# The gate of a gated unit as one silu on ScalarE in place of tanh and a VectorE product

## The chip, the cores and the metric

One core of a Trainium2 chip runs the whole program. The metric is the device time of one execution in microseconds (us), the median of several. Five engines work side by side, each through its own list in order: PE (TensorE, matrix products), DVE (VectorE), ACT (ScalarE), POOL (GpSimd) and SP (SyncE, which issues most DMAs).

## The reference

Three layers, one after the other, over 8 x 3072 = 24576 rows of 256 numbers:

```python
X = np.fft.rfft(x, axis=1)
y = np.fft.irfft(X * (filt_r + 1j * filt_i)[None], n=3072, axis=1)
...
out[do_compute] = xc + gate_w * (relu(xc @ w1[e]) @ w2[e])
...
rms = np.sqrt(np.mean(x * x, axis=-1, keepdims=True) + 1e-06)
xn = x / rms * rms_g
g = xn @ w_gate
silu = g * (1.0 / (1.0 + np.exp(-g)))
val = xn @ w_val
return (silu * val @ w_out).astype(np.float32)
```

The first layer is a filter by a Fourier transform, the second sends rows to one of eight experts, and the third, the gated unit with 1536 hidden channels, takes every row. The change lies in the third.

## The kernel before

The program has three stages: transform and routing, then the experts, then the gated unit (`glu`). `glu` takes the rows in 32 blocks of 768 and the hidden channels in 6 pairs of 256, so there are 192 pairs of work.

A pair makes two first products, g for the gate and v for the value, by a scheme of Winograd that needs seven products p1 to p7 of half size for each. Each product is three matmuls of fp16 parts (L1587) with 384 columns. They are summed in two kinds of PSUM bank: `psa` (p1, and on it p6, p7, p4; three buffers) and `psb` (p2 by itself, and p5 with p3 on it; two buffers). The quarters c11, c12, c22, c21 of a result arise on the way, and a further product may be added to a bank only when what was in it has been read:

- `copy` (L1594, ACT) takes p1, p5 and p1 + p6 out of their banks as s1, s5 and u2. p6 may go on p1 only after the first copy, p3 on p5 after the second, p7 after the third.
- `plus` (L1598, DVE) makes c11 = p2 + s1, c12 = (p5 + p3) + u2 and c22 = (p1 + p6 + p7) + s5 (rows gc<- or vc<-). p4 may go on its bank only after c22; then the bank holds c21.
- `gate` (L1603, ACT) makes t = tanh(g / 2) into a tile `th` of three buffers, and `gate2` (L1609, DVE) makes g = (1 + t) * g. For c21 the gate reads the bank.
- `hidden` (L1617, DVE) makes v * scale * g, `high` (L1627, ACT) its upper fp16 part hh, `low` (L1630, POOL) the lower one hl.

The second product (`stage_b`, L1674) multiplies hh and hl with the output weights, three matmuls of 256 columns for each of 12 groups of a pair, 18 slots behind the first. `finish` (L1687, ACT) takes a block's result out.

Beside this, `row_ops` makes the next block's rows: six squares on ACT (L777, first pair of a block), 1 / rms in tiny steps on DVE (L779, then L130, L132, L138, L139, L141 of `rsqrt_ops`), scalings on both (L790, L793), four sums on POOL (L804), the upper parts on ACT (L807), the lower on DVE (L809), and a transposing DMA (L812).

The order on each engine is written out by hand, slot by slot. 14 slots are a pair: a slot is one product, what follows it, one group of the second product, and a piece of the next rows. `place` gives the slots of the products (g: 0, 2, 3, 4, 5, 6, 8; v: 7, 9, 10, 11, 12, 13, 15 in the order p1 p2 p5 p6 p3 p7 p4; 15 lies in the next pair), and `plan` those of what follows:

```python
for n, k in (("c11", 4), ("c12", 7), ("c22", 8), ("c21", 9)):
    plan[k].append((gate, n))
    plan[k + 2].append((gate2, n))
for n, k in (("c11", 11), ("c12", 14), ("c22", 15), ("c21", 16)):
    plan[k].append((hidden, n))
    plan[k + 2].append((high, n))
    plan[k + 3].append((low, n))
```

An engine runs its list in this order, and an instruction that waits holds up all behind it on its engine.

Of the kernel before, what the change touches and what calls it, by code (L numbers as in the profile page):

```python
# [36 lines left out]
# the first expert's first AHEAD rows are fixed after FREEZE batches  # L37
# [4 lines left out]
def shape_constants():  # L42
    """Tables that depend on the shapes alone: the factors of the 3072-point
    transform (96 x 32), signs of the mirrored half, token numbers."""
# [54 lines left out]
    # tokens of a route step: transposed columns (n, t) in groups of 128  # L99
# [21 lines left out]
def rsqrt_ops(nc, pool, out, v, iters):  # L121
    """out ~ v ** -0.5 (v > 0): a bit-level first guess (3.5% off) and Newton steps; a list of
    instructions to emit in this order"""
# [28 lines left out]
def colsum(nc, psp, ones, v, n, tag="misc"):  # L152
    """Sum over the partitions of v [p, n], the same on every partition."""
    ps = psp.tile([128, 512], F32, tag=tag, name="colsum")
    nc.tensor.matmul(out=ps[:, :n], lhsT=ones[: v.shape[0]], rhs=v, start=True, stop=True)
    return ps[:, :n]


def fft_route(tc, x, filr, fili, w9, consts, y_dram, lst, lp, front, shared, then):
    """y_dram, lst, shared["basee"] from x; then: the parts of what comes next, taken one by one between  # L160
    the instructions of the steps behind the last of the first stage, which count from 0 on in
    shared["step"]. The pool front is theirs from 0 on, the left side's memory from 6 on; shared
    also has a pool and one of PSUM for small things."""
# [9 lines left out]
    with ExitStack() as ctx:  # L173
# [50 lines left out]
        # but for the first row of the lower half (in the first group) the halves are the same  # L224
# [21 lines left out]
        # every other group's matrix of the inverse is the transposed one of the forward  # L246
# [22 lines left out]
        # the places in the lists, of the batches until FREEZE and of the others  # L269
# [27 lines left out]
        # one-hot rows and a group of zeros behind them  # L297
# [86 lines left out]
        def stage1(s):  # L384
            """rows (k1, re/im) of the 96-point transforms -> DRAM"""
# [31 lines left out]
        def stage23(s):  # L417
            """32-point transforms, the filter, the inverse 32-point ones"""
# [46 lines left out]
        def stage4(s):  # L465
            """back to tokens"""
# [22 lines left out]
        def batch_scale(b):  # L489
            """s with |y| * s <= 60000: |y| <= max|F| * ||x_b||"""  # L490
# [15 lines left out]
        def route(s):  # L506
# [97 lines left out]
            def place():  # L604
# [12 lines left out]
                # the first expert's later tokens come behind its first AHEAD rows  # L617
# [42 lines left out]
        for s in range(steps + lagr + 3):  # L660
# [19 lines left out]
            # behind the last transforms nothing else hides the routes' waits  # L680
# [25 lines left out]
def split(nc, hi, lo, src, scale):  # L706
    """hi + lo = src * scale in two fp16 parts"""
    nc.scalar.activation(out=hi, in_=src, func=ACTF.Copy, scale=scale)
    nc.vector.scalar_tensor_tensor(
        out=lo, in0=src, scalar=scale, in1=hi, op0=ALU.mult, op1=ALU.subtract  # L710
    )


def decode64_ops(nc, pool, out, w):
    """out [128, n] = float64 values given as words w [128, n, (low, high)], rounded to float32
    (zero below its normal range); a list of instructions to emit in this order"""
# [7 lines left out]
        # sign, exponent and 20 bits  # L724
# [10 lines left out]
        # and the other 32  # L735
# [8 lines left out]
# The GLU's two products with the rows, C = A B, are made per pair of halves of the rows (A1, A2),  # L744
# of the channels and of 256 columns by Winograd's form of Strassen's scheme:
#   s1 = a21 + a22, s2 = s1 - a11, s3 = a11 - a21, s4 = a12 - s2
#   t1 = b12 - b11, t2 = b22 - t1, t3 = b22 - b12, t4 = b21 - t2
#   c11 = a11 b11 + a12 b21, u2 = a11 b11 + s2 t2, u3 = u2 + s3 t3
#   c12 = u2 + s1 t1 + s4 b22, c21 = u3 + a22 t4, c22 = u3 + s1 t1
# PA: the products' places in the order a22 a11 a12 s1 s2 s3 s4 (t4 b11 b21 t1 t2 t3 b22)  # L750
PA = dict(p1=1, p2=2, p3=6, p4=0, p5=3, p6=4, p7=5)
GH = 384
# slots between a pair's first product and its first in the second
BEHIND = 18
# slots by which the second block's rows come later than another block's
LATE = 14
# the slots of a block's steps towards the next one's rows: squares, 1 / rms (and how many apart),
# scalings (by whom: ScalarE or VectorE), sums, and per third the fp16 parts and what is left
# [8 lines left out]
def row_ops(nc, pool, x, xa, xs, xT, jk):  # L767
    """rows x [128, 6, D] over their rms, times XG (the first three of a partition are A1, the
    others A2) -> the seven factors in the tiles xa ([128, 3, 8, 128] or three of a third of it),
    their fp16 parts in xs, transposed  # L770
    in xT [128, 14 (hi, lo), GH]; a list of (slot of a block, instruction)"""
# [13 lines left out]
    # places of xa: a21, then those of PA  # L785
# [31 lines left out]
def block_list(nc, cp, basee, c_blk):  # L817
    """expert counts -> list of (expert, first slot) per block of TL slots behind every expert's
    first NSE blocks; the number of pairs of them; a list of instructions to emit in this order"""
# [28 lines left out]
    def loads():  # L848
# [16 lines left out]
        # n // 3 = n * 171 >> 9 for n < 512  # L865
# [11 lines left out]
        # the first block of an expert  # L877
# [13 lines left out]
        # entries behind the last block: the rows of the list that hold no token  # L891
# [16 lines left out]
def moe(tc, y_dram, lst, c_blk, w1, w2, wsp, lp, front, shared):  # L908
    """NSE blocks of TB list rows for every expert (rows without a token do nothing), then a
    loop over blocks of TL of what is left. The parts until the last yield make the first two  # L910
    blocks' rows and the first expert's weights and belong between the last steps of fft_route;
    after them shared["glu"] is what the GLU has to have made on the way."""
# [6 lines left out]
    # nothing before step n  # L919
# [32 lines left out]
    # the list of blocks from NS on: 0: expert, 1: row  # L952
# [13 lines left out]
    # a scale for w1 and one for w2 from their norms, to 0.2% (undone exactly in the end), and  # L966
    # the products' scale in 12
# [55 lines left out]
    with ExitStack() as ctx:  # L1023
# [5 lines left out]
        # ids of the next block but one  # L1029
        ids_n = cp.tile([128, 4, 2], I32, name="m_ids_n")  # L1030
        jk_x = cp.tile([128, D], F16, name="m_jkx")
        # state that goes from one turn of the loop to the next, empty at first
# [34 lines left out]
        # blocks from NS on come from the list  # L1067
# [12 lines left out]
        # n: sums of squares of the rows -> r: 1 / rms, to 0.2% (undone exactly in the end)  # L1080
# [27 lines left out]
        def stage_a(d, w_, f, T, busy=False):  # L1108
# [11 lines left out]
            # the sum is at most 16 XS TBIG  # L1120
# [37 lines left out]
        # tokens per partition in block j  # L1158
# [3 lines left out]
        # what block j does in its slot f for the blocks behind it  # L1162
        def step(j, u, f):
# [25 lines left out]
            # the first block's come late  # L1189
# [12 lines left out]
        # the next expert's weights  # L1202
# [14 lines left out]
        # what VectorE and ScalarE can do beside the block's own work in a slot, and what the  # L1217
        # weights take of it, in us
# [6 lines left out]
        def block(j, u, w, wp):  # L1225
# [4 lines left out]
            # GpSimdE still fills the lists in the first block  # L1230
# [74 lines left out]
        # the list of the blocks from NS on and the GLU's weights and first rows are made on the way  # L1305
        work, late, credit = [], [], [0.0, 0.0]

        def begin():
# [3 lines left out]
            # what they need is loaded some slots ahead  # L1312
# [9 lines left out]
        # the loop's first block ends one without tokens  # L1322
# [19 lines left out]
def glu_weights(gp, wg, wv, wo, rg):  # L1342
    """wg and wv (times rg) as the fp16 parts of the seven factors and wo as fp16 parts, under
    scales from their norms, and the first block's rows, in tiles of gp; w["work"](nc, ctx, tc,
    ps_m) lists (us, instruction) that make the weights, w["first"](nc, y_dram, room) then
    instructions for the rows"""
# [23 lines left out]
    def make(nc, ctx, tc, ps_m):  # L1370
# [34 lines left out]
        def scale(m, part):  # L1405
            """st 8-10: squares of norms; 11-13: 1 / norm; 14-16: scales; 17-19: inverses"""
# [26 lines left out]
        def columns(m, n, w):  # L1433
            pieces(m, [w[k * 128:(k + 1) * 128, c * 256:(c + 1) * 256]
                       for k in range(2) for c in range(NP)])
            # a column's norm is at most that of the rows' largest values
# [10 lines left out]
            # a factor is at most sqrt(8) times the norm  # L1447
# [51 lines left out]
        # 20: tanh's scale  # L1499
        one(20, 17, 0.5 / XG)  # L1500
        # h = (1 + tanh) * g * (v * st21) = silu * v * st22, at most TBIG
        mul(22, 11, 12)
        one(22, 22, 0.9 * TBIG / 256.0)
        mul(21, 17, 18)
        mul(21, 21, 22)
        one(21, 21, 0.5 / (XG * XG))
        # 23: the output's scale
# [7 lines left out]
def glu_rows(dram, i):  # L1515
    """(partitions, places, rows [partitions, places, D]) of block i; the first block has the
    tokens of the first step of the routes, which are among the first 768 of every list"""
# [11 lines left out]
def glu(tc, y_dram, w, out, ntok=NTOK):  # L1529
# [5 lines left out]
    with ExitStack() as ctx:  # L1535
# [32 lines left out]
        def stage_a(i, q):  # L1568
            """{slot: product}, {slot: what follows in it}"""
# [6 lines left out]
            # p1 + p6 + p7 + p4 and p5 + p3 are sums in one bank, read on the way  # L1576
# [23 lines left out]
            def gate(n):  # L1600
                z["t", n] = tile_("th", bufs=3)
                src = z["g", "p1" if n == "c21" else n]
                nc.scalar.activation(out=z["t", n], in_=src, func=ACTF.Tanh, scale=st[:, 20:21])  # L1603

            def gate2(n):
                src = z["g", "p1" if n == "c21" else n]
                if n == "c21":
                    z["g", n] = tile_("gc21")
                v.scalar_tensor_tensor(  # L1609
                    out=z["g", n], in0=z["t", n], scalar=1.0, in1=src, op0=ALU.add, op1=ALU.mult  # L1610
                )

            def hidden(n):
# [164 lines left out]
```

## Time and profile before

| | us |
|---|---|
| median of 3 runs | 3460.76 |
| lowest, highest | 3455.25, 3463.61 |
| span of the profiled execution, first to last instruction | 3426.4 |
| busy in the span: PE | 3207.6 (94%) |
| DVE | 2682.2 (78%) |
| ACT | 2284.5 (67%) |
| POOL | 1565.2 (46%) |

For the profiled execution the span is listed, and no total of its own; the runs' median is 34.4 us above that span. The shares are means over three stages of different kind: what the change does is read from the last one. A matmul's row begins when it starts to stream and ends, by a model, when its last result is out, so rows of neighbouring matmuls overlap. The granted clock of 1.00 is TensorE's upper level, 2.4 GHz.

### The profile page before, as it was taken

To read this page: it belongs to the slowest core of one execution; us is meant where nothing else is said; L and a number is where in the kernel's file an instruction comes from. 1 tells how busy PE (TensorE), PEld (TensorE's weight loads), DVE (VectorE), ACT (ScalarE), POOL (GpSimd) and SP (SyncE) were. 2 spreads that over 40 slices of the span, in tenths; PEclk is the share of its full clock that TensorE was granted. 3 is DMA by queue.
4 is the path that set the end of the run, shared out by engine and by line. 5 is a ranking of instruction groups with operands and counts; after the bars stand their busy time and mean duration, and the time that the engine had idled before them with its cause. 6 is when DMAs were issued, how large, how long until landed. Compare 5 with 4: busy or idle time off the path is not lost.

```text
span 3426.4 us, 61356 instructions
## 1 busy us (share of the span) xinstructions
PE 3207.6 (94%) x21784; PEld 2173.9 (63%) x21784; DVE 2682.2 (78%) x5587; ACT 2284.5 (67%) x4949; POOL 1565.2 (46%) x1546
## 2 busy tenths in 40 slices
PE   7888888889989988999999999999999999999999
PEld 3455555455555665666666666666666666666666
DVE  3666777698988656888888888888888888888886
ACT  5555655667676755776767777776677767767665
POOL 2355556756565643344343444334334443434433
PEclk8999998899999999999999999999999999999999
DMA  9999998555555462112111111111211111111110
GB/s 266 268 259 261 272 260 229 163 167 158 172 162 176 140 179 64 45 41 55 41 45 46 45 45 46 50 45 41 55 36 47 44 50 45 46 50 45 41 37 19
DMA packets 377758, 364.77 MB, mean 106 GB/s; under 512 B 264036, under 2 KB 323444, under 8 KB 373094
## 3 DMA queue, kind: packets, MB, share of 16 engines
q1 hardware_dynamic: 360502, 335.29, 35.8%
q0 software_dynamic: 16944, 25.51, 2.6%
q8 instruction: 173, 2.83, 0.3%
q14 instruction: 139, 1.14, 0.1%
HBM read 157.96 MB, written 133.80 MB: 85 GB/s over the span
## 4 chain that ended last, share of the span: by engine, by line
PE 52%; DVE 6%; ACT 2%; issue 1%; DMA 0%; DVEq 0%; POOL 0%; ACTq 0%; SPq 0%
PE psa L1587 19%; PE o L1674 18%; PE psb L1587 15%; DVE gc L1609 3%; DVE vc L1598 2%; ACT th L1603 1%; ACT s L1594 1%; DVE rsq_g L132 1%; DVE vc L1617 1%; DVE gc L1598 0%; PE m_o L1133 0%; DMA x<-y 0%; DMA xT<-xs 0%; DVE ss L779 0%; ACT hh L1627 0%
## 5 line engine op out<-in xcount | busy, mean ns | idle before, releaser
L1630 POOL TENSOR_TENSOR hl<-vc,hh 128x384 f16<-128x384 f32 x768 | 735.6, 961 | 1238.2 <-ACT hh L1627 1238.2
L1674 PE MATMUL o<-g_wo,hh 128*128 128x256 f16 x4608 | 878.9, 273 | 0.0
L1674 PEld LDWEIGHTS <-hh 128*128 128x128 f16 x4608 | 450.5, 98 | 296.8
L1674 PE MATMUL o<-g_wo,hl 128*128 128x256 f16 x2304 | 628.0, 273 | 0.1
L1627 ACT CAST hh<-vc 128x384 f16<-128x384 f32 x768 | 392.7, 511 | 162.4 <-DVE vc L1617 155.9
L1587 PE MATMUL psa<-xT,g_vhi 128*128 128x384 f16 x1488 | 484.1, 326 | 15.7 <-DVE vc L1598 15.6
L1587 PE MATMUL psa<-xT,g_ghi 128*128 128x384 f16 x1488 | 484.2, 326 | 0.8 <-DMA xT<-xs 0.5
L1617 DVE SCALAR_TENSOR_TENSOR vc<-vc,g_st,gc 128x384 f32<-128x384 f32 x576 | 405.5, 725 | 0.0
L1609 DVE SCALAR_TENSOR_TENSOR gc<-th,gc 128x384 f32<-128x384 f32 x576 | 392.4, 708 | 0.0
L1587 PE MATMUL psb<-xT,g_vhi 128*128 128x384 f16 x1116 | 363.0, 326 | 11.4 <-ACT s L1594 11.4
L1587 PEld LDWEIGHTS <-g_ghi 128*128 128x128 f16 x2688 | 263.1, 98 | 123.1 <-issue 0.3
L1603 ACT ACTIVATE th<-gc,g_st 128x384 f32<-128x384 f32 x576 | 338.5, 615 | 0.0
L1587 PE MATMUL psb<-xT,g_ghi 128*128 128x384 f16 x1116 | 332.8, 326 | 0.0
L1115 PE MATMUL psa<-m_xT,m_w 128*128 128x512 f16 (+1 forms) x1344 | 318.7, 377 | 10.1 <-DMA m_xT<-m_xs 8.7
L1587 PEld LDWEIGHTS <-g_vhi 128*128 128x128 f16 x2688 | 262.7, 98 | 102.6
L1133 PE MATMUL m_o<-m_w,m_hh 128*128 128x256 f16 x1740 | 304.8, 277 | 11.7 <-PEq L1336 10.1
L1594 ACT COPY s<-psb 128x384 f32<-128x384 f32 x384 | 183.5, 478 | 171.1 <-PE psb L1587 171.1
L1594 ACT COPY s<-psa 128x384 f32<-128x384 f32 x384 | 182.9, 476 | 164.5 <-PE psa L1587 164.4
L1133 PE MATMUL m_o<-m_w,m_hl 128*128 128x256 f16 x870 | 241.2, 277 | 44.2 <-POOL m_hl L1126 32.2
L1587 PE MATMUL psa<-xT,g_glo 128*128 128x384 f16 x744 | 242.5, 326 | 0.0
L1674 PEld LDWEIGHTS <-hl 128*128 128x128 f16 x2304 | 225.4, 98 | 26.7 <-POOL hl L1630 0.6
L1587 PE MATMUL psa<-xT,g_vlo 128*128 128x384 f16 x744 | 242.4, 326 | 0.0
(255 smaller groups left out, 6521.2 us busy)
## 6 DMA issues: line engine op xcount, KB each, us to landing
x<-in_x_dram SPq DMA_DIRECT2D x64, 384.0 KB
a_d<-a SPq DMA_DIRECT2D x64, 384.0 KB
a<-a_d SPq DMA_DIRECT2D x128, 192.0 KB
b_d<-bt SPq DMA_DIRECT2D x128, 192.0 KB
b<-b_d SPq DMA_DIRECT2D x32, 768.0 KB
y<-y SPq DMA_DIRECT2D x64, 384.0 KB
x<-y SPq DMA_DIRECT2D x28, 768.0 KB
out_dram<-ot SPq DMA_DIRECT2D x27, 768.0 KB
```

The costliest lines, as they stand in the source:

```text
L132: lambda: ve.tensor_scalar(out=g, in0=g, scalar1=-1.0, scalar2=float(0x5F3759DF), op0=ALU.mult, op1=ALU.add),
L1115: nc.tensor.matmul(out=ps, lhsT=w[:, k, fs], rhs=d["xT"][:, o + k, 0:n], start=(j == 0), stop=(j == 5),)
L1133: nc.tensor.matmul(out=o[t // 2][:, t % 2, :], lhsT=h[:, ts_], rhs=w_["w2"][:, f, i, :], start=(f == k == t % 2 == 0), stop=(f == KF - 1 a ...
L1587: nc.tensor.matmul(out=ps, lhsT=w_[m][:, q, k, :], rhs=xT[:, o + k, :], start=(j == 0 and bank == p), stop=(j == 2), skip_group_check=True,)
L1594: nc.scalar.copy(out=z[m, n], in_=z[m, p])
L1598: v.tensor_tensor(out=z[m, n], in0=z[m, p], in1=z[m, b], op=ALU.add)
L1603: nc.scalar.activation(out=z["t", n], in_=src, func=ACTF.Tanh, scale=st[:, 20:21])
L1609: v.scalar_tensor_tensor(out=z["g", n], in0=z["t", n], scalar=1.0, in1=src, op0=ALU.add, op1=ALU.mult)
L1617: v.scalar_tensor_tensor(out=z["v", n], in0=src, scalar=st[:, 21:22], in1=z["g", n], op0=ALU.mult, op1=ALU.mult,)
L1627: nc.scalar.copy(out=part(hh, n), in_=z["v", n])
L1630: nc.gpsimd.tensor_tensor(out=part(hl, n), in0=z["v", n], in1=part(hh, n), op=ALU.subtract)
L1674: nc.tensor.matmul(out=o_t[b][:, t % 2, :], lhsT=h[:, f, ts_], rhs=wo16[:, 2 * q + f, k, :], start=(j == 0 and q == 0 and n == first_of[b] ...
```

## The change

The gate becomes one ScalarE activation, silu(g) = g * sigmoid(g), written over g (for c21 into the same tile as before). The tanh, its tile `th` and the VectorE product are gone. The scalars beside it change with it: silu takes the whole argument, so its scale is twice tanh's, and the factor st21 of `hidden` no longer carries g's scale. In the listing after, lines behind the gate lie up to eight higher: `copy` is L1593, `plus` L1597, `hidden` L1609 and `high` L1619.

```diff
-        # 20: tanh's scale
-        one(20, 17, 0.5 / XG)
-        # h = (1 + tanh) * g * (v * st21) = silu * v * st22, at most TBIG
+        one(20, 17, 1.0 / XG)
         mul(22, 11, 12)
         one(22, 22, 0.9 * TBIG / 256.0)
-        mul(21, 17, 18)
-        mul(21, 21, 22)
-        one(21, 21, 0.5 / (XG * XG))
+        mul(21, 18, 22)
+        one(21, 21, 1.0 / XG)
...
             def gate(n):
-                z["t", n] = tile_("th", bufs=3)
-                src = z["g", "p1" if n == "c21" else n]
-                nc.scalar.activation(out=z["t", n], in_=src, func=ACTF.Tanh, scale=st[:, 20:21])
-
-            def gate2(n):
                 src = z["g", "p1" if n == "c21" else n]
                 if n == "c21":
                     z["g", n] = tile_("gc21")
-                v.scalar_tensor_tensor(
-                    out=z["g", n], in0=z["t", n], scalar=1.0, in1=src, op0=ALU.add, op1=ALU.mult
-                )
+                nc.scalar.activation(out=z["g", n], in_=src, func=ACTF.Silu, scale=st[:, 20:21])
...
                 plan[k].append((gate, n))
-                plan[k + 2].append((gate2, n))
```

On VectorE, in the first pair of a block where the 1 / rms of the next rows begins, the order before (with the semaphores that each instruction waits for):

```order
L1609 SCALAR_TENSOR_TENSOR gc_25118<-th,gc_25118 128x384 [waits Activation_49]
L1598 TENSOR_TENSOR vc_25190<-psb,s_25168 128x384 [waits PE_49,Activation_49,Pool_49]
L1609 SCALAR_TENSOR_TENSOR gc_25148<-th,gc_25148 128x384 [waits Activation_49]
L1609 SCALAR_TENSOR_TENSOR gc_25157<-th,gc_25157 128x384 [waits Activation_49]
L1609 SCALAR_TENSOR_TENSOR gc_25214<-th,psa 128x384 [waits Activation_49]
L1617 SCALAR_TENSOR_TENSOR vc_25190<-vc_25190,g_st,gc_25118 128x384 [waits DVE_49]
L779 TENSOR_SCALAR ss<-ss 128x6 [waits Activation_49]
L130 TENSOR_SCALAR rsq_g<-ss 128x6 [waits DVE_49]
L1598 TENSOR_TENSOR vc_25225<-psb,u_25212 128x384 [waits PE_49,Activation_49,Pool_49]
L132 TENSOR_SCALAR rsq_g<-rsq_g 128x6 [waits DVE_49]
L138 TENSOR_TENSOR rsq_a<-rsq_g 128x6 [waits DVE_49]
L1598 TENSOR_TENSOR vc_25235<-psa,s_25202 128x384 [waits PE_49,Pool_49]
```

and at the same place in the change:

```order
L1597 TENSOR_TENSOR vc_24657<-psb,s_24637 128x384 [waits PE_49,Activation_49,Pool_49]
L1609 SCALAR_TENSOR_TENSOR vc_24657<-vc_24657,g_st,gc_24589 128x384 [waits DVE_49]
L779 TENSOR_SCALAR ss<-ss 128x6 [waits Activation_49]
L130 TENSOR_SCALAR rsq_g<-ss 128x6 [waits DVE_49]
L1597 TENSOR_TENSOR vc_24688<-psb,u_24677 128x384 [waits PE_49,Activation_49,Pool_49]
L132 TENSOR_SCALAR rsq_g<-rsq_g 128x6 [waits DVE_49]
L138 TENSOR_TENSOR rsq_a<-rsq_g 128x6 [waits DVE_49]
L1597 TENSOR_TENSOR vc_24698<-psa,s_24668 128x384 [waits PE_49,Pool_49]
```

The four products of L1609 before are gone, and everything behind them keeps its place relative to the rest.

On ScalarE, behind the upper part L807 of the next rows in a later pair, the order before:

```order
L807 CAST xs<-xa 128x896
L1594 COPY s_20514<-psa 128x384 [waits PE_49]
L1603 ACTIVATE th<-gc_20494,g_st 128x384 [waits DVE_49]
L1603 ACTIVATE th<-gc_20504,g_st 128x384 [waits DVE_49,Activation_49]
L1603 ACTIVATE th<-psa,g_st 128x384 [waits DVE_49,PE_49]
L1594 COPY s_20547<-psb 128x384 [waits PE_49]
L1594 COPY u_20556<-psa 128x384 [waits PE_49]
```

and in the change:

```order
L807 CAST xs<-xa 128x896
L1593 COPY s_20239<-psa 128x384 [waits PE_49,Activation_49]
L1603 ACTIVATE gc_20220<-gc_20220,g_st 128x384 [waits DVE_49]
L1603 ACTIVATE gc_20230<-gc_20230,g_st 128x384 [waits DVE_49]
L1603 ACTIVATE gc_20260<-psa,g_st 128x384 [waits PE_49]
L1593 COPY s_20269<-psb 128x384 [waits PE_49,Activation_49]
L1593 COPY u_20277<-psa 128x384 [waits PE_49,Activation_49]
```

The gates stand where they stood and wait for less; 867 of the 1152 copies now also wait for an earlier instruction of ScalarE itself. At the start of the unit the order has one instruction more:

```order
L1593 COPY u_15548<-psa 128x384
L1603 ACT_TABLE_LOAD
L1603 ACTIVATE gc_15537<-gc_15537,g_st 128x384
L1593 COPY s_15565<-psa 128x384
L1603 ACTIVATE gc_15554<-gc_15554,g_st 128x384
```

That load is the only one in the unit; before, the whole program has one, at its beginning.

## Rows read from the trace of the kernel before

**Rows 1.** Windows: stretch and length, busy PE, PEld, DVE, ACT, POOL, clock, DMA.
```profile
1400.00:3300.00 1900.00, 1873.91 (x13470) 1316.77 (x13469) 1586.55 (x2967) 1344.19 (x3024) 783.61 (x804) 1.00 0.18 46
3285.00:3293.00 8.00, 8.00 (x60) 5.67 (x59) 6.00 (x13) 7.59 (x21) 2.17 (x4) 1.00 0.00 0
```

**Rows 2.** Lines by form, DVE, 1400 to 3300: busy us, mean ns, idle before.
```profile
L1609 DVE SCALAR_TENSOR_TENSOR gc<-th,gc 128x384 f32<-128x384 f32 x518 | 352.9, 708 | 0.0
```

**Rows 3.** Lines by form, ACT, 1400 to 3300.
```profile
L1603 ACT ACTIVATE th<-gc,g_st 128x384 f32<-128x384 f32 x518 | 304.5, 615 | 0.0
```

**Rows 4.** Who waited for whom, PE, 1400 to 3300: total us, times, longest.
```profile
PE psa L1587 <- DVE vc L1598: 15.1, 30, 0.8
PE psb L1587 <- ACT s L1594: 10.6, 28, 0.9
```

**Rows 5.** Chain in order of time, last block: start us, us, what.
```profile
3382.39 0.97 PE psb L1587 x6
...
3403.90 0.97 PE psb L1587 x6
```

**Rows 6.** Timeline, PE: one product, and the same one a block later.
```profile
3251.73 0.33 PE L1587 MATMUL psb<-xT,g_ghi 128*128 128x384 f16 x1
...
3317.69 0.33 PE L1587 MATMUL psb<-xT,g_ghi 128*128 128x384 f16 x1
```

**Rows 7.** Timeline, all engines, first pair of that block.
```profile
3291.80 0.48 ACT L1594 COPY u<-psa 128x384 f32<-128x384 f32 x1
3291.88 0.32 PE L1587 MATMUL psb<-xT,g_vhi 128*128 128x384 f16 x1
3292.41 0.51 ACT L1627 CAST hh<-vc 128x384 f16<-128x384 f32 x1
3292.44 0.17 DVE L130 TENSOR_SCALAR rsq_g<-ss 128x6 int32<-128x6 int32 x1
3292.55 0.56 DVE L1598 TENSOR_TENSOR vc<-psb,u 128x384 f32<-128x384 f32 x1
3293.00 0.91 POOL L1630 TENSOR_TENSOR hl<-vc,hh 128x384 f16<-128x384 f32 x1 [4.64 <-ACT hh L1627]
3293.02 0.92 DVE L132 TENSOR_SCALAR rsq_g<-rsq_g 128x6 int32<-128x6 int32 x1
3294.05 0.55 DVE L1598 TENSOR_TENSOR vc<-psa,s 128x384 f32<-128x384 f32 x1
3294.66 0.32 PE L1587 MATMUL psa<-xT,g_vhi 128*128 128x384 f16 x1 [0.50 <-DVE vc L1598]
```

**Rows 8.** Timeline, ACT and PE, two pairs later.
```profile
3302.96 0.48 ACT L1594 COPY u<-psa 128x384 f32<-128x384 f32 x1 [0.25 <-PE psa L1587]
3304.26 0.51 ACT L1627 CAST hh<-vc 128x384 f16<-128x384 f32 x1 [0.82 <-DVE vc L1617]
3311.14 0.94 ACT L807 CAST xs<-xa 128x896 f16<-128x896 f32 x1 [1.43 <-POOL xa L804]
3313.84 0.47 ACT L1594 COPY s<-psb 128x384 f32<-128x384 f32 x1
3314.36 0.32 PE L1587 MATMUL psb<-xT,g_vhi 128*128 128x384 f16 x1 [0.36 <-ACT s L1594]
```

**Rows 9.** Timeline: releases by PE of DVE and ACT, and of PE.
```profile
3289.37 0.33 PE L1587 MATMUL psb<-xT,g_vhi 128*128 128x384 f16 x1
3289.84 0.56 DVE L1598 TENSOR_TENSOR vc<-psb,s 128x384 f32<-128x384 f32 x1 [1.07 <-PE psb L1587]
3307.16 0.33 PE L1587 MATMUL psb<-xT,g_ghi 128*128 128x384 f16 x1
3307.52 0.48 ACT L1594 COPY s<-psb 128x384 f32<-128x384 f32 x1 [0.80 <-PE psb L1587]
3308.14 0.33 PE L1587 MATMUL psb<-xT,g_ghi 128*128 128x384 f16 x1
```

**Rows 10.** Timeline, ACT, start of the program.
```profile
0.73 1.28 ACT L401 ACT_TABLE_LOAD   x1 [0.73 <-PEq L1767]
```

## The prediction, made before the changed kernel was run

> **What bounds the kernel now.** I read the busy times by stage first, then who waited for whom on PE, then the timeline of one block. The change touches only the gated unit, which fills the last three fifths of the span. In its steady part [rows 1] PE is busy for 1873.9 of 1900 us at a granted clock of 1.00, DVE for 1586.6 and ACT for 1344.2. So the unit is bound by PE, and all that a lighter DVE can give back is time in which PE is not streaming. The waits of PE [rows 4] name 15.1 us for DVE (30 times) and 10.6 us for ACT (28 times): once each per block of rows.
>
> How much is lost in all comes from the pace. Two pairs that nothing disturbs take 3403.90 - 3382.39 = 21.51 us, so 10.755 a pair and 64.53 for the six of a block [rows 5]. A block that also prepares the next one's rows takes 3317.69 - 3251.73 = 65.96 [rows 6]. Each of the 31 such blocks (the last prepares nothing) loses 1.43 us, 44 us together. This is more than the waits listed, since after a wait PE also has to refill: 10.755 us for 42 matmuls of 384 and 36 of 256 columns make 0.163 for one of the first kind, while its row is 0.33 long [rows 7]. In a stream the rest lies under the next matmul; after a wait 0.16 is lost besides. The wait of 0.50 ahead of 3294.66 costs 0.66.
>
> **Where the 1.43 us arise.** First place [rows 7]: PE's p4 of the value half waits for VectorE's sum at 3294.05, which stands behind the tiny L132 of the rsqrt. L132 is 0.92 us long and ends 0.03 after POOL's hl at 3293.00, though its neighbour L130 of the same size takes 0.17: it is held by POOL. Second place [rows 8]: p3 waits for ACT's copy at 3313.84 to 3314.31. ACT was late because L807 waited 1.43 us for POOL's sums; that costs PE the wait of 0.36 and the same 0.16 of refill, 0.52. The other 0.25 are small delays around both.
>
> **The change part by part.** PE, POOL and SP keep their instructions and their order. (a) *768 products (1 + t) * g leave VectorE*, three in four of them from SBUF at 708 ns in the mean [rows 2], 353 us in the steady part. That lies beside PE, and is worth only what it takes from the two places.
>
> Second place: POOL's chain begins with hl of c11, which needs ACT's hh at 3304.26. That hh waited 0.82 for VectorE's hidden product, which stood behind three of the removed products. Without them it follows copy u, which ends at 3303.44 [rows 8]. POOL's chain, L807 and the copy start about 0.8 earlier. The lateness is 0.52, so it goes: -0.52 x 31 = **-16.1** (0 if POOL's chain does not follow, -16.1 at most).
>
> First place: the sum cannot start before L132 ends, and L132 ends with POOL's hl. hl follows hh at 3292.41, which follows copy u (end 3292.28, the earliest that hh can gain is 0.13, and about 0.24 where neighbours on ACT overlap). L132 itself can come 0.2 earlier at best, since the sum ahead of it needs PE's matmul of 3291.88 (end 3292.20, release 0.14 as in [rows 9], so 3292.34 in place of 3292.55). Both move by nearly the same amount, and POOL was ahead by 0.02 and stays so. So I take the wait as shortened, not gone: -0.2 x 31 = **-6.2**; its ends are 0 and -0.66 x 31 = -20.5. The Trainium skill (SBUF — State Buffer, SBUF: two separate sides) says that of such a pair whichever starts first holds the port for the whole instruction; by it the end is decided by these hundredths, and -20.5 would hold if L132 came first. The row of L132 agrees with it.
>
> Small delays: of the 0.25 I take half, -0.12 x 31 = **-3.7** (0 to -7.8).
>
> (b) *Silu in place of tanh, 768 times.* The operands are the same, the result goes to g itself. No row has a silu; the nearest is tanh of the same shape at 615 ns [rows 3], and I take **0** more. The lower end is the plain copy's 0.48 us [rows 9], the upper end tanh's time twice.
>
> (c) *One table load*, ahead of the first silu, where ACT has little ahead and PE waits soon: 1.28 us in the only row there is [rows 10], **+1.3**. By the Trainium skill (ScalarE: Activation LUTs, What ACT_TABLE_LOAD costs) a switch has a drain of about 1.38 us besides, so 2.66; the row shows the load alone, with nothing in flight ahead of it. By the page the sum would be 1.4 us less of a gain.
>
> (d) *A second wait on ACT's copies.* In the order of the change 867 of the 1152 copies out of PSUM wait for PE and for ACT itself, where each waited for PE alone. What ACT is waited for lies far back; the cost is that two waits release later. ACT's copy at 3307.52 started 0.03 after PE's last matmul (3307.16 + 0.33), VectorE's sum with several waits at 3289.84 started 0.14 after its own (3289.37 + 0.33) [rows 9]: 0.11 more. It hurts where a copy has little slack: the copy that ends at 3308.00 releases p3 of the gate half at 3308.14, and the release takes 0.05 (3314.31 to 3314.36, [rows 8]), so the slack is 0.09. That leaves 0.02 in each of 192 pairs, 3.8 us; VectorE's row has more waits than ACT's will, so I take half, **+2** (0 to 0.11 x 192 = 21). What is queued behind the copies on ACT are gates and casts, and PE waits for the copies alone.
>
> (e) One scalar product less in the constants: a 1-column VectorE instruction in the stage before, under PE's work there, 0; without that cover below 0.2.
>
> Sum: -16.1 - 6.2 - 3.7 + 1.3 + 2 = **-22.7 us**. The profile's span of 3426.4 would be 3403.7. The profiled execution's total time is not listed; between its span and the median of 3460.76 lie 34.4 us, which I leave as they are: 3438 us, 0.66% less. About 0.3% (10.4 us) is what a measurement of this kernel can tell from no change.
>
> **The rivals.**
> *L132 gets ahead of POOL.* Then the first place gives 20.5 in place of 6.2 and the time is 3460.8 - 37 = **3424**. For it: the two are within 0.05 us by the working above. Against it: POOL is ahead in this block by 0.02, and 30 waits of 0.50 in the mean [rows 4] say the same of the others.
> *The gain is given back at the copies.* If the second wait costs its full 0.11 in each pair, (d) is 21 and the time **3457**; if POOL's chain does not come earlier, -16.1 falls out and it is **3454**. Both end within 0.3%. For it: the slack of 0.09 is in every pair, and POOL's own work ahead of L807 stays as long as it is. Against it: the slack is there, and hh is named as waiting for VectorE.
> *Silu is longer than tanh, and ACT becomes the bound.* In the first pair of a block ACT has squares and outputs besides and is busy for 7.59 of 8 us [rows 1]; four gates lie in that stretch ahead of the value half's copy for p3. Each added x delays PE by 4x per block: with x of 0.18 the 22.7 are gone (4 x 31 x 0.18 = 22.3), and with x of 0.6, twice tanh, the time is 3438 + 74 = **3512**. For it: there is no row of a silu. Against it: copy and tanh of one shape are only 0.14 apart [rows 3, 9]. The Trainium skill (ScalarE: Activation LUTs, Step-by-step) has one element per cycle for every function, by which x is 0; no run here shows it.
> *The change does not do what it says*: if silu, square and copy needed different tables, loads would come in turn, six squares a block between gates. The order has one load in the whole unit, so this has no share of its own.
>
> **How the numbers follow.** My forecast 0.50; L132 first 0.26; given back 0.17; ACT as the bound 0.07. The range is 3416 to 3452: the forecast with the ends of its small terms, and the first rival with 8 us below it, where small delays go too. Faster by over 0.3% 0.79, within 0.3% 0.14, slower 0.07.
>
> **What would show it.** In the profile after: PE's wait for ACT's copy near each block's L807 gone, and L807's wait for POOL under 1 us; PE's wait for VectorE's vc sum still there once a block at about 0.3 (gone: the first rival); DVE busy near 60% in the steady part (83% now); silu from SBUF at 615 ns; one table load more; blocks at 65.2 us. Wrong would be: blocks of 65.9 or more, waits of PE for the copies in each pair, or gates above 0.7 us.

## The result, and the profile after

The changed kernel takes 3434.68 us (median of 4 runs, 3429.15 to 3438.36); the kernel before takes 3462.19 in the runs beside it (4 runs, 3455.25 to 3465.99). The ratio is 0.9917, with an interval of 0.9901 to 0.9933. It is faster by 27.5 us, where 22.7 were forecast, and the time lies 3.3 us below the forecast of 3438.

First the busy times by stage, over the same stretch as in [rows 1] (stretch and length, then busy PE, PEld, DVE, ACT and POOL, the granted clock, DMA):

```profile
1400.00:3300.00 1900.00, 1891.16 (x13639) 1333.77 (x13637) 1219.98 (x2305) 1340.17 (x3068) 762.17 (x815) 1.00 0.19 46
```

DVE has lost 367 us of its 1587, PE has gained 17, and ACT is where it was. The granted clock is at its upper level in both. So only a small part of the work taken from VectorE comes back, and to see where, one reads who waited for whom (us in all, times, longest). After the change, first PE, then ACT:

```profile
PE psa L1586 <- DVE vc L1597: 8.6, 30, 0.6
...
ACT xs L807 <- POOL xa L804: 14.9, 29, 0.8
ACT hh L1619 <- DVE vc L1609: 10.8, 30, 0.6
```

The same two waits of ACT in the kernel before:

```profile
ACT hh L1627 <- DVE vc L1617: 138.5, 204, 1.5
...
ACT xs L807 <- POOL xa L804: 40.8, 28, 2.1
```

Of PE's two waits of [rows 4] the one for ACT's copy is gone, and the one for VectorE's sum is shortened from 15.1 to 8.6 us. On ACT, L807's wait for POOL is 0.5 us a block, where it was 1.4 to 1.5.

The timeline of a block's first pair, all engines, at the place of [rows 7] (start, us, engine, line, operation; in brackets the idle time before and what ended it):

```profile
2318.69 0.48 ACT L1593 COPY u<-psa 128x384 f32<-128x384 f32 x1
2319.04 0.17 DVE L130 TENSOR_SCALAR rsq_g<-ss 128x6 int32<-128x6 int32 x1
2319.05 0.54 ACT L1619 CAST hh<-vc 128x384 f16<-128x384 f32 x1
2319.66 0.92 POOL L1622 TENSOR_TENSOR hl<-vc,hh 128x384 f16<-128x384 f32 x1 [4.42 <-ACT hh L1619]
2319.73 0.87 DVE L132 TENSOR_SCALAR rsq_g<-rsq_g 128x6 int32<-128x6 int32 x1
2320.72 0.56 DVE L1597 TENSOR_TENSOR vc<-psa,s 128x384 f32<-128x384 f32 x1
2321.33 0.32 PE L1586 MATMUL psa<-xT,g_vhi 128*128 128x384 f16 x1 [0.28 <-DVE vc L1597]
```

L132 still takes 0.87 us for six numbers per partition, and still ends within 0.02 of POOL's hl (2320.60 and 2320.58). The sum ahead of p4 starts 1.06 after hl's start, as it did before (1.05). What moved is hl: it starts 0.97 after the start of copy u, where it was 1.20. PE's wait is 0.28 in place of 0.50.

The timeline of ACT two pairs later, at the place of [rows 8]:

```profile
2329.69 0.48 ACT L1593 COPY u<-psa 128x384 f32<-128x384 f32 x1 [0.31 <-PE psa L1586]
2330.07 0.52 ACT L1619 CAST hh<-vc 128x384 f16<-128x384 f32 x1
...
2336.94 0.94 ACT L807 CAST xs<-xa 128x896 f16<-128x896 f32 x1 [0.50 <-POOL xa L804]
...
2339.64 0.47 ACT L1593 COPY s<-psb 128x384 f32<-128x384 f32 x1
```

The cast hh follows copy u at once, where it waited 0.82. L807 starts 7.25 after copy u (8.18 before), and the copy that p3 waits for is 0.93 earlier with it. 0.52 were lost there, so nothing is left of that wait.

The gate itself, lines by form on ACT in that stretch (count, then busy us and mean ns):

```profile
L1603 ACT ACTIVATE gc<-gc,g_st 128x384 f32<-128x384 f32 x525 | 308.8, 616 | 0.0
```

Silu takes 616 ns where tanh took 615 [rows 3]. And the start of the unit on ACT, with the one new table load:

```profile
1336.09 0.48 ACT L1593 COPY u<-psa 128x384 f32<-128x384 f32 x1
1336.59 1.28 ACT L1603 ACT_TABLE_LOAD   x1
1337.88 0.62 ACT L1603 ACTIVATE gc<-gc,g_st 128x384 f32<-128x384 f32 x1
```

**What the total is made of.** This execution took 3432.34 us and its span is 3430.5: 1.9 us lie around a span. The profile of before has a span of 3426.4, so its execution took about 3428, less than any of the listed runs of that kernel. The unit explains it: its first matmul starts at 1302.88 in the profile before and at 1333.55 in the one after. From there to the end it takes 3426.4 - 1302.88 = 2123.5 before and 3430.5 - 1333.55 = **2097.0 after, 26.5 less**. The two stages in front, which the change does not touch, took 31 us more in the second execution, and two spans compared as they stand would have shown a slower kernel. In the rest of this document I compare the length of the unit, and the period of a block by the distance of two L132: 65.97 before, 65.15 after (medians).

### The profile page after: what moved, and what is told of

It reads as the page before. It is cut to its first block, busy times and chain, and to the rows that moved or that the text cites. A ratio compares the mean times of both kernels' runs of the same rounds, so it can differ in the third digit from the quotient of the medians.

```text
span 3430.5 us, 61136 instructions
## 1 busy us (share of the span) xinstructions
PE 3211.9 (94%) x21784; PEld 2179.3 (64%) x21784; DVE 2257.9 (66%) x4818; ACT 2260.9 (66%) x4950; POOL 1529.9 (45%) x1546
## 4 chain that ended last, share of the span: by engine, by line
PE 56%; ACT 3%; DVE 1%; DMA 0%; issue 0%; DVEq 0%; SPq 0%; ACTq 0%
PE psa L1586 21%; PE o L1665 20%; PE psb L1586 16%; ACT gc L1603 1%; ACT jk L777 1%; DVE vc L1597 1%; ACT s L1593 1%; ACT hh L1619 0%; DVE rsq_g L132 0%; ACT ot L1678 0%; ACT u L1593 0%; DMA x<-y 0%; PE m_o L1133 0%; DMA xT<-xs 0%; DVE ss L779 0%
## 5 line engine op out<-in xcount | busy, mean ns | idle before, releaser
L1622 POOL TENSOR_TENSOR hl<-vc,hh 128x384 f16<-128x384 f32 x768 | 700.3, 915 | 1247.3 <-ACT hh L1619 1247.3
L1619 ACT CAST hh<-vc 128x384 f16<-128x384 f32 x768 | 394.2, 513 | 14.1 <-DVE vc L1609 13.9
L1609 DVE SCALAR_TENSOR_TENSOR vc<-vc,g_st,gc 128x384 f32<-128x384 f32 x576 | 379.2, 681 | 5.7
L1593 ACT COPY s<-psa 128x384 f32<-128x384 f32 x384 | 183.0, 477 | 296.3 <-PE psa L1586 296.2
L1603 ACT ACTIVATE gc<-gc,g_st 128x384 f32<-128x384 f32 x576 | 338.7, 616 | 0.0
L1593 ACT COPY s<-psb 128x384 f32<-128x384 f32 x384 | 183.5, 478 | 201.9 <-PE psb L1586 201.7
L1597 DVE TENSOR_TENSOR vc<-psb,s 128x384 f32<-128x384 f32 x192 | 106.6, 555 | 197.1 <-PE psb L1586 195.1
```

The source lines that it names most:

```text
L1593: nc.scalar.copy(out=z[m, n], in_=z[m, p])
L1597: v.tensor_tensor(out=z[m, n], in0=z[m, p], in1=z[m, b], op=ALU.add)
L1603: nc.scalar.activation(out=z["g", n], in_=src, func=ACTF.Silu, scale=st[:, 20:21])
L1609: v.scalar_tensor_tensor(out=z["v", n], in0=src, scalar=st[:, 21:22], in1=z["g", n], op0=ALU.mult, op1=ALU.mult,)
L1619: nc.scalar.copy(out=part(hh, n), in_=z["v", n])
L1622: nc.gpsimd.tensor_tensor(out=part(hl, n), in0=z["v", n], in1=part(hh, n), op=ALU.subtract)
```

## The experiments

The experiments ran on three chips, each with runs of the kernel before on it. The table has all of them; ratios are to the kernel before on the same chip. Unit and block are in us, each from one profiled execution.

| kernel | median, before beside it | ratio [interval] | unit | block |
|---|---|---|---|---|
| before, once more | 3441.24, 3439.86 | 1.0003 [0.9993, 1.0013] | 2123.5 | 65.97 |
| silu, and a product | 3437.94, 3439.86 | 0.9989 [0.998, 0.9999] | 2122.9 | 65.97 |
| tanh in silu's place | 3413.05, 3439.86 | 0.9913 [0.9898, 0.9928] | 2096.4 | 65.15 |
| before, one product earlier | 3441.87, 3467.58 | 0.9922 [0.9902, 0.9941] | 2097.6 | 65.15 |
| after, 1 / rms later | 3436.98, 3439.86 | 0.9993 [0.9984, 1.0002] | 2123.4 | 66.00 |
| before, 1 / rms later | 3489.12, 3467.58 | 1.0062 [1.0043, 1.0081] | 2142.4 | 66.6 |
| before, one product earlier and 1 / rms later | 3468.09, 3467.58 | 0.9998 [0.9987, 1.0009] | 2122.7 | 66.0 |
| after, L132 earlier | 3395.98, 3438.18 | 0.989 [0.9871, 0.9908] | 2083.5 | 64.71 |
| before, product and L132 earlier | 3426.07, 3438.18 | 0.9963 [0.9949, 0.9977] | 2111.5 | 65.63 |

### The kernel before, once more

No edit.

> The kernel before, unchanged, to see where its 3460 us lie: the profile read for the prediction has a span of 3426.4 us and was taken to have 34 us around it, while the changed kernel's runs have their total only 1.9 us above their span. If the 34 us lie around the span, the unit starts near 1303 us as in the profile before and the total is 34 us above the span. If that profile was of an execution with a short first stage, the unit starts near 1330 us, the total is 2 us above the span, and the unit itself takes 2123 us in both.

The total of its profiled execution is 3441.79 at a span of 3439.9, again 1.9 apart. The unit starts at 1316.36, 13.5 later than in the first profile, and takes 2123.5, the same to 0.1. So what lies around the span is small, and what differs between executions of one program lies in the stages ahead of the unit. Most of that goes with the chip: the kernel before has medians of 3438, 3440 and 3468 us on the three.

### Silu with a product behind it

The gate writes silu into a tile of its own, and VectorE makes src * 0 + silu at the place of the old product: the same operation, shape and order as before, with the function of the change on ScalarE. The lines are shown against the kernel before; the scalars are those of the change.

```diff
-                nc.scalar.activation(out=z["t", n], in_=src, func=ACTF.Tanh, scale=st[:, 20:21])
+                nc.scalar.activation(out=z["t", n], in_=src, func=ACTF.Silu, scale=st[:, 20:21])
...
-                    out=z["g", n], in0=z["t", n], scalar=1.0, in1=src, op0=ALU.add, op1=ALU.mult
+                    out=z["g", n], in0=src, scalar=0.0, in1=z["t", n], op0=ALU.mult, op1=ALU.add
```

> The changed kernel with silu written to a tile of its own and a VectorE product of the old size put back (0 * g + silu, two slots behind the gate). If the gain comes from VectorE's queue alone, both waits of PE return: blocks of 65.96 us, a total within 0.3% of the kernel before. If silu itself, the single table load or the lighter waits of the gates gave part of it, the total stays below, at 3435 to 3450 us.

The gain is gone: 2122.9 us of unit against 2123.5. Both waits of PE are back at their sizes of [rows 4]; waits of PE and of ACT, 1400 to 3300:

```profile
PE psa L1586 <- DVE vc L1597: 14.3, 29, 0.5
PE psb L1586 <- ACT s L1593: 11.0, 29, 0.9
...
ACT xs L807 <- POOL xa L804: 42.1, 29, 2.0
```

So the gain does not come from the other function, but goes with VectorE's product. One part of ScalarE's side is undone here too: the copies start 0.04 us after PE's last matmul, as in the kernel before, where most of them take 0.09 after the change. This run alone does not part that second wait from the product; the run with one product moved does, since its copies also start after 0.04.

### Tanh in silu's place

The changed kernel with the name of the function alone exchanged, so that the gate is tanh(g) and no product follows (the factor g is left out).

```diff
-                nc.scalar.activation(out=z["g", n], in_=src, func=ACTF.Silu, scale=st[:, 20:21])
+                nc.scalar.activation(out=z["g", n], in_=src, func=ACTF.Tanh, scale=st[:, 20:21])
```

> The changed kernel with tanh in place of silu (the gate is then tanh of the scaled g, without the product with g). If silu costs what tanh costs, blocks are 65.15 us and the total is that of the changed kernel, 3435 us, less 1.3 us for the table load that is not needed. If silu's rows are longer, this is faster by 4 x 31 x the difference.

A block takes 65.15 us with either function, and the unit 2096.4 against 2097.0. This kernel has one ScalarE instruction less, the table load. So silu costs what tanh costs, and the load of 1.28 us costs the unit 0.6 at most. At the end of the second pair nothing of it is left: PE begins the value half's p4 of the second pair 20.53 us after the unit's first matmul with the load (1354.08 - 1333.55) and 20.55 without (1338.23 - 1317.68).

### Before, with one product moved

Is it the 367 us of work, or the place of one product a pair behind that work? This is the kernel before with tanh, all products and their order, but with the hidden product of c11 at slot 9, ahead of three gate products, in place of slot 11 behind them.

```diff
+            plan[9].append((hidden, "c11"))
...
-                plan[k].append((hidden, n))
+                if n != "c11":
+                    plan[k].append((hidden, n))
```

> The kernel before with the hidden product of c11 two slots earlier, ahead of three of the four products (1 + t) * g; VectorE's work is the same. If PE's wait for ACT's copy arises because this product starts POOL's chain late, the wait goes: 0.52 x 31 = 16 us less, 3445 us, and L807's wait for POOL falls from 1.4 to about 0.6 us. If it is VectorE's load beside POOL that slows POOL's sums, L807 still waits 1.4 us and the total is that of before.

The block takes 65.15 us and the unit 2097.6: all but 0.6 us of the change's gain, with VectorE still busy for 1550 of 1900 us. VectorE's timeline in a pair, and below it the waits of PE and ACT, 1400 to 3300:

```profile
2319.19 0.56 DVE L1598 TENSOR_TENSOR vc<-psb,s 128x384 f32<-128x384 f32 x1 [1.07 <-PE psb L1587]
2319.78 0.62 DVE L1617 SCALAR_TENSOR_TENSOR vc<-vc,g_st,gc 128x384 f32<-128x384 f32 x1
2320.32 1.02 DVE L1609 SCALAR_TENSOR_TENSOR gc<-th,gc 128x384 f32<-128x384 f32 x2
2321.25 0.55 DVE L1609 SCALAR_TENSOR_TENSOR gc<-th,psa 128x384 f32<-128x384 f32 x1
```

```profile
PE psa L1587 <- DVE vc L1598: 8.5, 29, 0.8
...
ACT xs L807 <- POOL xa L804: 14.7, 29, 0.5
ACT hh L1627 <- DVE vc L1617: 11.0, 30, 0.5
```

The hidden product stands right behind the sum that it needs. The wait of hh for it, 138.5 us in 204 times in the kernel before, falls to 11.0 in 30, POOL's chain comes earlier, and with it L807 and the copy: the chain that the prediction gave for the second place, moved by its first link alone. I had expected only that place to be gained; the first is shortened too, since the same hh sets hl there. L132 starts 0.38 after hl in this kernel, takes 0.56 and again ends with it, and the sum starts 1.06 after hl's start, as before and after the change.

### Three ways of moving the 1 / rms that gained nothing

If POOL's hl holds L132 up, then steps of 1 / rms that come two slots later should miss it. The edit is one number, made in the changed kernel, in the kernel before, and in the kernel before with the product moved:

```diff
-RMS, APART = 11, 0.5
+RMS, APART = 13, 0.5
```

> The changed kernel with the tiny rsqrt steps two slots later (RMS 13), so that VectorE makes the sum that p4 waits for before it comes to L132, which POOL holds. If what is left of PE's wait for VectorE is POOL's hold on L132, that wait (0.28 listed, 0.43 lost per block) is gone: blocks of 64.7 us and a total 13 us lower, 3422 us. If the wait is VectorE's load or release, it stays and the total stays at 3435 us.

> The kernel before, tanh and product kept, with the rsqrt steps two slots later. If PE's wait for VectorE there is POOL's hold on L132 and not the 768 products, this wait goes without the change: 0.66 x 31 = 20 us less, 3440 us, while the wait for ACT's copy stays at 0.36 a block. If it is the load of the products, the wait stays and the total is that of before.

> Both moves on the kernel before, with tanh and all products kept. If the 768 products cost nothing beside PE and mattered only by their two places, this loses as little as the changed kernel with its rsqrt steps later: blocks of 64.8 us, 3425 us or less. If VectorE's load matters in itself, it stays above the changed kernel, 3435 us.

All three miss the time that was expected. L132 takes 0.17 us in each, and the wait for the value half's sum is gone (in one of the three, one of 0.2 us is left). In its place stands a longer one. The changed kernel with this edit, waits of PE from 1500 to 3350:

```profile
PE psa L1586 <- DVE gc L1597: 35.0, 28, 1.3
```

and its timeline, all engines:

```profile
2376.43 1.79 POOL L1622 TENSOR_TENSOR hl<-vc,hh 128x384 f16<-128x384 f32 x2 [2.49 <-ACT hh L1619]
2376.82 0.55 DVE L138 TENSOR_TENSOR rsq_a<-rsq_g 128x6 f32<-128x6 f32 x1
2377.40 0.84 DVE L139 SCALAR_TENSOR_TENSOR rsq_a<-rsq_a,ss 128x6 f32<-128x6 f32 x1
2378.52 0.91 POOL L1622 TENSOR_TENSOR hl<-vc,hh 128x384 f16<-128x384 f32 x1 [0.29 <-ACT hh L1619]
2378.68 0.77 DVE L139 SCALAR_TENSOR_TENSOR rsq_a<-rsq_a,ss 128x6 f32<-128x6 f32 x1
2380.11 0.55 DVE L1597 TENSOR_TENSOR gc<-psa,s 128x384 f32<-128x384 f32 x1
2380.72 0.32 PE L1586 MATMUL psa<-xT,g_ghi 128*128 128x384 f16 x1 [1.25 <-DVE gc L1597]
```

The later steps of the rsqrt now meet the next three hl. Two end with them to 0.02 (2378.24 and 2378.22; 2379.45 and 2379.43), and behind them stands the sum that frees the bank of the gate half's p4. That is a wait of 1.25 us a block, more than was saved: the changed kernel's unit goes back from 2097.0 to 2123.4. In the kernel before, where the place at the copies is still lost too, it makes the unit 18.9 us longer. Two slots on, the tiny steps meet POOL again; what counts is where each of them stands.

### L132 ahead of hl

So the first steps alone were moved, by one slot: L132 and the first L138 stand with L130, ahead of the sum that they followed, and all others stay. This was done in the changed kernel, and in the kernel before with the product moved.

```diff
-    ops += [(RMS + int(i * APART), fn) for i, fn in enumerate(small)]
+    ops += [(RMS + (int(i * APART) if i > 3 else 0), fn) for i, fn in enumerate(small)]
```

> The changed kernel with two of the tiny rsqrt steps (L132 and the one behind it) one slot earlier, ahead of the sum that they stood behind; the later steps stay where they were. If the rest of PE's wait for VectorE is that POOL starts 0.07 us ahead of L132, L132 now comes first, takes 0.17 and the wait is gone (0.43 a block): blocks of 64.7 us, a unit of 2084 us, 13 us under the changed kernel, ratio to the kernel before 0.988. If the hold only moves to the next step, as it did with all steps two slots later, the blocks stay at 65.2 us or get longer.

> The kernel before, tanh and all 768 products kept, with the hidden product of c11 two slots earlier and L132 one slot earlier. If the order alone decides, as the unit of 2097.6 us with the first move says, this gains the same 13 us as the changed kernel does: a unit of 2084 us, ratio 0.988. If VectorE's greater load (83% of the steady part against 64%) makes L132 late here, the wait stays and the unit takes 2097 us.

In the changed kernel, all engines of a first pair, and its stretch:

```profile
2352.87 0.17 DVE L132 TENSOR_SCALAR rsq_g<-rsq_g 128x6 int32<-128x6 int32 x1
2353.08 0.17 DVE L138 TENSOR_TENSOR rsq_a<-rsq_g 128x6 f32<-128x6 f32 x1
2353.18 0.56 DVE L1597 TENSOR_TENSOR vc<-psb,u 128x384 f32<-128x384 f32 x1
2353.28 0.91 POOL L1622 TENSOR_TENSOR hl<-vc,hh 128x384 f16<-128x384 f32 x1 [4.41 <-ACT hh L1619]
2353.66 0.55 DVE L1597 TENSOR_TENSOR vc<-psa,s 128x384 f32<-128x384 f32 x1
2354.51 0.33 PE L1586 MATMUL psa<-xT,g_vhi 128*128 128x384 f16 x1
```

```profile
1400.00:3300.00 1900.00, 1899.73 (x13737) 1342.85 (x13736) 1216.76 (x2314) 1346.75 (x3080) 766.57 (x821) 1.00 0.19 46
```

L132 starts 0.41 ahead of hl and takes 0.17. The sum starts 0.38 after hl's start in place of 1.06, p4 does not wait, and the list of PE's waits is empty: PE is busy for 1899.73 of 1900 us. The unit takes 2083.5 us, 13.5 less than after the change; 31 blocks by 0.28 of wait and 0.16 of refill are 13.6. By the unit this version beats both kernels; its ratio to the kernel before is 0.989, 42 us.

In the kernel before with its product moved the same edit loses. Its timeline, and PE's waits, 1400 to 3300:

```profile
2310.53 0.55 DVE L1609 SCALAR_TENSOR_TENSOR gc<-th,psa 128x384 f32<-128x384 f32 x1
2311.00 0.17 DVE L779 TENSOR_SCALAR ss<-ss 128x6 f32<-128x6 f32 x1
2311.39 0.91 POOL L1630 TENSOR_TENSOR hl<-vc,hh 128x384 f16<-128x384 f32 x1 [4.41 <-ACT hh L1627]
2311.41 0.93 DVE L132 TENSOR_SCALAR rsq_g<-rsq_g 128x6 int32<-128x6 int32 x1
2312.95 0.55 DVE L1598 TENSOR_TENSOR vc<-psa,s 128x384 f32<-128x384 f32 x1
2313.55 0.32 PE L1587 MATMUL psa<-xT,g_vhi 128*128 128x384 f16 x1 [0.76 <-DVE vc L1598]
```

```profile
PE psa L1587 <- DVE vc L1598: 22.0, 29, 1.0
```

Here the gate products are in front of the tiny steps. L779 starts when the last of them lets it, L132 comes 0.01 after hl's start (10 ns in the trace) and is held, and now two sums stand behind it in place of one. The block is 0.48 us longer than without the edit. This is the one place where the lighter VectorE was worth something that this move of the hidden product does not give: room for L132 ahead of hl.

How close the two run shows in the same profile. In 27 of the 31 blocks L132 starts 5 to 12 ns after hl by the trace and is held, 0.93 us in all. In two it starts 3 and 4 ns after it and takes 0.17; there hl takes 0.94 in place of 0.91, and the hold falls on L138 behind it:

```profile
1786.54 0.94 POOL L1630 TENSOR_TENSOR hl<-vc,hh 128x384 f16<-128x384 f32 x1 [4.42 <-ACT hh L1627]
1786.55 0.17 DVE L132 TENSOR_SCALAR rsq_g<-rsq_g 128x6 int32<-128x6 int32 x1
1786.75 0.76 DVE L138 TENSOR_TENSOR rsq_a<-rsq_g 128x6 f32<-128x6 f32 x1
```

## Why the prediction was right

The sign, the size and the mechanism hold. The terms around the two places were sized less well: 3.3 us of costs came to nothing, and the small delays gave 1.5 less than forecast, so these errors cancel in part. By its own steps:

- *Second place, -16.1.* It held. The wait for ACT's copy is gone from the list, and both the silu with a product and the single moved product show that it hangs on what stands ahead of the hidden product on VectorE. The two runs of the kernel before with 1 / rms later, without and with the product moved, price the place: PE waits 36.2 us in 29 times for the gate's sum in both, the wait for the copy (10.7 us) is in the first alone, and the block falls from 66.60 to 66.00. That is 0.60, the 0.52 and a part of the small delays.
- *First place, -6.2.* The wait was forecast as shortened to about 0.3 and still there, and is 0.28. With 0.16 of refill the place costs 0.44 in place of 0.66, 0.22 x 31 = 6.8. The argument was that hl and L132 move by nearly the same amount and POOL stays ahead: hl moved by 0.23 against copy u, and its lead over L132 went from 0.02 to 0.07. The Trainium skill (SBUF — State Buffer, SBUF: two separate sides) calls the port pair that VectorE and GpSimd share an exclusive lock: of a GpSimd operation that reads SBUF and a VectorE one in a two-port mode or with two SBUF inputs, whichever starts first has it for the whole instruction. The runs agree, to within 4 ns: started 0.07 after hl, L132 takes 0.87 us; 0.01 after it, 0.93; 0.41 ahead of it, 0.17, and the wait is gone.
- *Small delays, -3.7.* Of a block's loss against 64.53, 65.15 - 64.53 = 0.62, 0.44 is the first place, so 0.18 is left of 0.25: 0.07 x 31 = 2.2.
- *Silu, 0.* 616 ns against 615.
- *The table load, +1.3.* At most 0.6 by the run with tanh, and nothing is left of it at the end of the second pair. The row has 1.28 between a copy that ended 0.02 before and a gate that starts 0.01 after, so the drain of about 1.38 that the Trainium skill (ScalarE: Activation LUTs, What ACT_TABLE_LOAD costs) adds does not appear beside it.
- *A second wait on ACT's copies, +2.* It measured nothing. The copy at 2334.25 is released 0.09 after p5's last matmul (0.03 in [rows 9]) and ends at 2334.73; p3 starts at 2334.81, in the stream. Its slack of 0.09 became 0.03, once the release of 0.05 is taken off: the delay of 0.06 is inside it. No wait of PE for a copy is in the list, and the kernel with one product moved, whose copies wait once, has the same block of 65.15.

```profile
2333.83 0.33 PE L1586 MATMUL psb<-xT,g_ghi 128*128 128x384 f16 x1
...
2334.81 0.33 PE L1586 MATMUL psb<-xT,g_ghi 128*128 128x384 f16 x1
```

```profile
2334.25 0.48 ACT L1593 COPY s<-psb 128x384 f32<-128x384 f32 x1 [0.77 <-PE psb L1586]
```

The three terms together are 16.1 + 6.8 + 2.2 = 25.1 us, which is 31 x (65.96 - 65.15), of the unit's 26.5. Of the other 1.4, 0.6 lie in the first block, where the distance of two L132 falls from 55.87 to 54.47, 1.40 in place of 0.81. Most of the rest lies in blocks that were longer than the median before (up to 66.9) and are less so now (up to 65.5).

Three statements were off. The 34.4 us "between its span and the median" do not lie around the span; 1.9 do, and the rest was that the profiled execution had shorter stages ahead of the unit than the listed runs. It did no harm, because the sum was made of differences in the unit, and the unit had the same length in both executions of before. VectorE was forecast near 60% in the steady part and is at 64%: the rows of neighbours overlap (the sum of 2319.26 takes 0.56, and the next starts 0.47 later), so taking a row out lowers the busy time by less than its length. And the picture of the first place was too simple: it is not one instruction that POOL holds but whichever of the tiny steps comes beside an hl.

The rival *L132 gets ahead of POOL* did not come about by the change, but it came about by one slot's move on top of it: 2123.5 - 2083.5 = 40.0 us of gain, where the rival had 37.

What stays open is why the stages ahead of the unit take up to 48 us more in one execution than in another (the unit starts at 1302.88 in one profile and at 1351.26 in another). The traces show where a part of it lies. In the four profiles whose unit starts after 1330, PE waits once for 10 to 17 us for VectorE's L578 of the routing, near 660 to 690, and the granted clock over 600 to 900, a mix of its two levels, is 0.87 to 0.91. In the other seven that wait is below 3 us and the clock 0.95 to 0.97. Three of the four ran on the chip where the kernel before takes 3468 us. Why VectorE comes late there was not followed.

## What to carry to other kernels

Work that is taken from an engine beside the bound one was worth here what it moved at the places where the bound engine waits: one product a pair, moved ahead of three, gave what the removal of four a pair gave, to 0.6 us. The emptier engine then had room for a further move, worth 13.5 us, that lost time on the fuller one. So follow each wait of the bound engine back to the instruction that stands at the head of a line, and ask what it stands behind. A tiny instruction in front of a release can be that one: where another engine can hold it, what starts first decides (0.17 us against 0.93 here), and it is worth placing by hundredths of a microsecond. Compare stages by their own length, since spans of two executions can differ by more than the change in stages that it does not touch.

## What the runs showed of the hardware

- A VectorE step on six numbers per partition takes 0.17 us, or as long as POOL's two-input operation beside it has left, up to 0.93. This holds for L132, L138 and L139. Started 3 or 4 ns after POOL's, L132 was not held, and POOL's operation took 0.94 in place of 0.91; from 5 ns on it was. A sum with one input in PSUM is not held: the one at 2353.66 keeps its 0.55 inside POOL's 0.91.
- With two semaphores to wait for, an ACT copy is released 0.09 us after PE's last matmul, in place of 0.03 to 0.04 with one.
- A table load between other work on ACT took 1.28 us and 0.03 around it; at the end of the second pair PE was where it was without the load.
